# A one-core attention and Fourier-mixing kernel: a small addition moved from VectorE to GpSimd, and a few steps of a written-out order moved

## The chip, the cores and the metric

The kernel runs on one core of a Trainium2 chip. A core has TensorE (PE, matrix products into PSUM), VectorE (DVE), ScalarE (ACT), GpSimd (POOL) and SyncE (SP), each with its own queue that it works through in order, and 16 DMA engines. The metric is the time of one execution on the device, in microseconds. Before the change the median of three runs is 413.38 us (412.26 to 414.96).

## The reference

Inputs are q, k and v, each 8 batches x 8 heads x 576 rows x 64, a projection w_phi (64 x 128) and two weights of a feed-forward layer (512 x 2048 and 2048 x 512), all float32.

```python
def phi(x):
    proj = np.einsum('bhsd,df->bhsf', x, w_phi)
    proj = proj - np.max(np.abs(proj), axis=-1, keepdims=True)
    return np.concatenate([np.exp(proj), np.exp(-proj)], axis=-1)
q_p, k_p = (phi(q), phi(k))
kv = np.einsum('bhsf,bhsd->bhfd', k_p, v)
z = np.sum(k_p, axis=2)
num = np.einsum('bhsf,bhfd->bhsd', q_p, kv)
den = np.einsum('bhsf,bhf->bhs', q_p, z)[..., None] + 1e-06
x = (num / den)            # heads side by side: 8 x 576 x 512
mixed = np.real(fft(fft(x, axis=1), axis=2))
u = x + mixed
un = (u - mean(u)) / np.sqrt(var(u) + 1e-06)     # over the 512 columns
out = u + np.maximum(un @ w_ch1, 0.0) @ w_ch2
```

## The kernel before, in words

**Tiling.** A batch has 576 rows: chunks 0 to 3 of 128 rows and chunk 4 of 64 rows. k and q are loaded by GpSimd's DMAs (with a cast to bf16), transposed by DMAs that SyncE issues, and multiplied with w_phi on TensorE. ScalarE takes both exponentials of each product (KPp and KPn of keys, QPHP and QPHN of queries) out of PSUM, and VectorE takes the maxima of its absolute values (MK of keys, MQ of queries). In place of being subtracted, k's maximum is an exponential factor on v: ScalarE writes it into column 64 of VCn, VCp (and V4N, V4P of the 64 rows), and GpSimd multiplies v by it (lines 441 and 426).

TensorE then makes kv for each head and, for each head in the order 0, 1, 6, 7, 4, 5, 2, 3, the numerators and denominators (pn_, line 953). VectorE combines the two signs (tg, line 960, then cb, line 967) and takes a reciprocal per pair of heads (rd, line 971); GpSimd multiplies the pair into X (line 973). There are two cb buffers.

The Fourier transforms are products with sine and cosine tables, made small by symmetry: VectorE first folds X by rows into R (`folded`, lines 867 to 891), then by columns (CEO), TensorE multiplies twice (psD, pu), and VectorE adds the result to X. ScalarE writes X minus its mean into UN, SyncE's DMAs transpose that to UT, TensorE makes the hidden layer (psf, line 1211), ScalarE its relu HT (lines 1216 and 1218), TensorE the output (pso, lines 1228 and 1255), and VectorE adds it, times the row's scale, to X (lines 1234 and 1262). SyncE stores X to the output (lines 1187 to 1198).

**The row's scale.** `scales` makes 1/sqrt(var + 1e-6) for the five chunks of a batch from the variances in MV: VE is the sum (line 1170), rs its power of -0.5 (line 1171, GpSimd). For batch 0 this is done in two parts, so there are nine such pairs of instructions. rs is read by the updates at lines 1234 and 1262.

**PSUM.** The pool pj has two buffers, for psk (keys), psq and psh (queries), psD and pn_; the pool pb has three, for psf, pso, pu and others; the pool pk has one. A new tile waits until all readers of the one before it in its buffer are done. Where two engines read the same PSUM tile, the second one in program order waits for the first, as the waits in the rows below show.

**What sets the order.** The table PLAN is a string of letters, one for each step of a stream; `step` takes the letter's stream one `yield` further, and each engine's queue is filled in that order. Each stream goes through the batches on its own: F is the feed-forward part, M the heads and the mixing, D the row folds (its first step is the first two folds), N the normalisation, U the scales, P the maxima of q, T the projections with their exponentials, R the maxima of k (its first step is the 64 rows, then one for each pair of heads), S the scaled v, K, V and Q the loads, A the transposes of q, B those of k, O the stores (its steps are chunks 2, 1, 3 and 4). At any time several batches are in work: while F of batch 3 runs, M works on batch 4 and T on batch 5.

The fetch of v (`fetch_v`) has three steps: the two loads of the 64 rows (VS4), then two of 4 heads each. v has one buffer, k's and q's transposes have one each, X has three.

Of the kernel before, what the change touches and what calls it, by code (L numbers as in the profile page):

```python
# [10 lines left out]
ALU = mybir.AluOpType  # L11
# [15 lines left out]
    "MFPTMMFOTFSFMPTFFOPTTPMFFFFMFSNBFMFPTQMFFAFMNPFTFMNMFFMFFMMFTTFFURMFFVFRMFFSTFFMFFMFVFTTPFFOFFRFPDFF"  # L27
    "FTPFFFFFVDDRFFFQFDTMTFFKKQTSMFFFMFFFMRMFTTTMMFNNOFFMMFMFMFFSSMTFMTFFFNOFOSQTPPMFTFMBFPTFPAMFFFMFNTFK"
    "MMFFFNFMFMFFMFFUMQMFFVMFFFTTPFFFFMTFFRFTTFFOVFFFRFFRFDFFFFDFDFFDPTFMFTTFFFFMKFRFTMSFMRFFOMFTSPMFNTMP"
    "NSQFFFFQMMMMTTTFFOBMSFFFFOTPMTFSFFMFFMTPVMFFFFMTPNFFNNMMMFFMAFFFMUFMFKMFFFMFFTTDTTFRFFSFFFFRVFFOTMFF"  # L30
    "FFFRPTFFDFFFDRFFFTDFMFVKTPFFFFFMTMBQMFFRSFMFOTSTSTMMFFFNNSFMMFMMFTFMFOPTMKKFFFFOPTPMTFFMFFFNMFTPPMFF"
    "FTNFQMNMVFFMFQMFMFFMUFFMFFVMAFFFFTTTTFDRFRFFTFSFFFOFMRFFQFFFDFFTFFFDFFRFVDFTFMFFTTMFFMFFMFRSMFOQTTTM"
    "FTQFNFMSFFMFFTNPMMFOMSTPMTFFFFOSMTPPMFTFFMPPFBAFMFPFMFNNFMMVVFMFMFFFMTTFRMNUFFFFFMRFFFMFFFSTFFMFFPTF"
    "FOTFFFDDFFFRFTFFFDFDVRFFFMFTTFFMFMTMFRFFSMFFSFOMTTNTFFMFNMMFFFMMFTFOMPSTFNFFFOPTFMFFTMPFFFFMPSPMFFTM"
    "FFPFTMNFFFNMFMFFFUMFMFMFFFFMFFMFMFFFFOFDFFDFFFFFDFFFDFMFFFMFMFFMMFFMFNFMNFFOFFFFMFFFFOFMNFFFOMFFNFFF"
    "FFFFFFFFFFFFNUFFFFFFFFFFFFFFFFFFFFFFFFFFFFFFFFFFFFFFFFFFFFFFFFFFF"
# [4 lines left out]
def kernel(  # L41
# [10 lines left out]
    nc = tc.nc  # L52
# [1098 lines left out]
    def measure(b, c):  # L1151
        X, mv, _ = mixed[b]
        M = rows(c)
        st = small.tile([128, 6], F32, tag="st", name="st")
        nc.vector.bn_stats(out=st[0:M, :], in_=X[0:M, c, 0:C])  # L1155
        nc.vector.bn_aggr(out=mv[0:M, c, :], in_=st[0:M, :])  # L1156

    def scales(b):
        mv = mixed[b][1]
        for first, cs in ((True, slice(0, 3, 2)), (False, slice(0, 5))):  # L1160
            if b == 0:
                for c in (0, 2) if first else (1, 3, 4):
                    measure(b, c)
                    yield
            if b and first:
                continue
            n = 2 if first else 5
            rs = small.tile([128, n], F32, tag=f"rs{n}", name=f"rs{n}")
            VE = small.tile([128, n], F32, tag=f"VE{n}", name=f"VE{n}")
            nc.vector.tensor_single_scalar(out=VE[:], in_=mv[:, cs, 1], scalar=1e-06, op=ALU.add)  # L1170
            nc.gpsimd.tensor_tensor(out=rs[:], in0=VE[:], in1=mhalf[:, 0:n], op=ALU.pow)  # L1171
            for j, c in enumerate((0, 2) if first else range(5)):
                if b or first or c in (1, 3, 4):
                    scale_of[b, c] = rs[:, j:j + 1]
            yield
# [163 lines left out]
    def fold_later(b):  # L1339
        yield from folds[b]  # L1340

    STREAMS = {
        "F": (forward, 68), "M": (mixing, 26), "D": (fold_later, 4), "N": (normalise, 5),
        "U": (scales, 1), "P": (part(0), 7), "T": (part(1), 18), "R": (part(2), 5),
        "S": (part(3), 5), "K": (fetch_k, 2), "V": (fetch_v, 3), "Q": (fetch_q, 3),
        "A": (arrive, 1), "B": (arrive_k, 1), "O": (store_all, 4), "W": (load_ffn_weights, 2),
# [55 lines left out]
```

## Time and profile before

| | |
|---|---|
| median of three runs | 413.38 us (412.26 to 414.96) |
| the profiled execution | 413.93 us, of it 412.2 us span from its first to its last instruction |
| granted TensorE clock, mean | 0.989 |
| DMA traffic | 42.71 MB, 104 GB/s in the mean |

The profile is that of one execution. Engine rows give the start and the length of an instruction, or of several alike in a row (x2, x4), and in brackets how long the engine had been idle before and what ended that. Names stand as out<-in with buffer numbers left out. A matmul's length is that of a pipeline: several overlap.

### The profile page before, as it was taken

The page shows a single profiled execution, that of the slowest core. Times are in us where ns is not written, and L with a number is a line of the kernel's source. Part 1 is how long each engine was busy: PE and PEld are TensorE (multiplying, and loading weights), DVE is VectorE, ACT ScalarE, POOL GpSimd, SP SyncE. Part 2 cuts the span into 40 slices and gives each one's busy share as a digit, 9 for nine tenths or more (in the row PEclk, how much of TensorE's full clock was granted, in tenths as well). Part 3 has the DMA queues.
Part 4 walks back from the last instruction along what each step waited for, and adds up shares of the span by engine and source line. Part 5 has one row for each costly group of instructions (what it writes and reads, how often), then busy time and mean ns, then how long its engine had stood idle before and what let it go on. Part 6 is the DMA issues. An engine that isn't in the chain of part 4 may idle for free.

```text
span 412.2 us, 10494 instructions
## 1 busy us (share of the span) xinstructions
PE 392.6 (95%) x4165; PEld 260.1 (63%) x4194; DVE 319.9 (78%) x662; ACT 303.6 (74%) x617; POOL 214.5 (52%) x279
## 2 busy tenths in 40 slices
PE   6898999999999998999999999999989999999995
PEld 3574476545856576566856577566846587657564
DVE  5889887999699887798689869788789768966102
ACT  7788999668958895598968886889758886444350
POOL 8898785765466753707658474647452342201000
PEclk9899899999999999999999999999999999999999
DMA  8979979998574959763985959756993150106202
GB/s 225 234 125 165 173 97 195 86 122 140 101 119 59 109 106 133 97 99 78 106 126 76 154 95 154 76 65 113 117 102 52 29 100 21 26 4 113 60 25 65
DMA packets 108674, 42.71 MB, mean 104 GB/s; under 512 B 82769, under 2 KB 103633, under 8 KB 108625
## 3 DMA queue, kind: packets, MB, share of 16 engines
q0 software_dynamic: 46272, 16.60, 37.2%
q1 hardware_dynamic: 61905, 25.11, 33.4%
q8 instruction: 33, 0.54, 0.5%
q10 hardware_dynamic: 448, 0.33, 0.3%
q14 instruction: 16, 0.13, 0.1%
HBM read 36.77 MB, written 9.44 MB: 112 GB/s over the span
## 4 chain that ended last, share of the span: by engine, by line
PE 76%; DVE 16%; DMA 3%; POOL 2%; issue 1%; ACT 1%; DVEq 0%; POOLq 0%
PE psf L1211 29%; PE pso L1228 20%; PE kv L851 4%; PE pso L1255 3%; PE psD L1033 2%; DMA KT<-KS 2%; PE pu L1085 2%; PE psh L561 2%; PE psk L466 2%; PE psq L520 2%; DVE R L867 2%; DVE MK L486 1%; DVE cb L967 1%; PE idle L1333 1%; DVE tg L960 1%
## 5 line engine op out<-in xcount | busy, mean ns | idle before, releaser
L1211 PE MATMUL psf<-UT,W1b 128*128 128x320 bf16 (+1 forms) x1024 | 141.1, 286 | 0.4 <-DMA UT<-UN 0.3
L1228 PE MATMUL pso<-W2b,HT 128*128 128x512 bf16 x467 | 117.0, 379 | 1.8 <-issue 0.6
L1211 PEld LDWEIGHTS <-W1b 128*128 128x128 bf16 x1024 | 94.7, 98 | 28.1 <-issue 2.4
L1216 ACT ACTIVATE HT<-psf 128x320 bf16<-128x320 f32 x128 | 53.8, 443 | 25.6 <-PE psf L1211 19.5
L1228 PEld LDWEIGHTS <-HT 128*128 128x128 bf16 x496 | 45.2, 98 | 43.1 <-issue 0.4
L973 POOL TENSOR_TENSOR X<-cb,rd 128x640 f32<-128x640 f32 x28 | 35.1, 1254 | 46.4 <-DVE rd L971 19.5
L441 POOL TENSOR_TENSOR VCn<-VS,VCn 128x512 bf16<-128x512 bf16 x28 | 29.6, 1059 | 45.2 <-ACT VCn L436 40.0
L528 DVE TENSOR_REDUCE MQ<-psq 128x8 f32<-128x1024 f32 (+1 forms) x32 | 34.3, 1088 | 14.8 <-PE psq L520 14.4
L1234 DVE SCALAR_TENSOR_TENSOR X<-pso,rs,X 128x512 f32<-128x512 f32 x31 | 23.1, 744 | 28.2 <-PE pso L1228 28.0
L1218 ACT ACTIVATE HT<-psf 128x512 bf16<-128x512 f32 x64 | 37.4, 602 | 4.8 <-PE psf L1211 4.5
L486 DVE TENSOR_REDUCE MK<-psk 128x8 f32<-128x1024 f32 x28 | 33.8, 1210 | 1.4 <-ACT KPn L472 1.4
L472 ACT ACTIVATE KPp<-psk 128x1024 bf16<-128x1024 f32 x28 | 28.7, 1027 | 8.3 <-PE psk L466 8.2
L258 POOL DMA_DIRECT2D QS<-in_q_dram x49 | 33.5, 691 | 1.1 <-DMA QT<-QS 0.6
L1131 ACT ACTIVATE UN<-X,MV 128x512 bf16<-128x512 f32 (+1 forms) x35 | 25.2, 726 | 11.7 <-DVE MV L1156 8.1
L570 ACT ACTIVATE QPHP<-psh 128x1024 bf16<-128x1024 f32 x28 | 28.9, 1031 | 4.3 <-PE psh L561 4.0
L472 ACT ACTIVATE KPn<-psk 128x1024 bf16<-128x1024 f32 x28 | 28.7, 1024 | 2.1 <-DVE MK L486 2.1
L441 POOL TENSOR_TENSOR VCp<-VS,VCp 128x512 bf16<-128x512 bf16 x28 | 29.6, 1057 | 0.0
L570 ACT ACTIVATE QPHN<-psh 128x1024 bf16<-128x1024 f32 x28 | 29.0, 1034 | 0.0
L1155 DVE BATCH_NORM_STATS2 st<-X 128x6 f32<-128x512 f32 (+1 forms) x40 | 27.1, 678 | 0.2
L1075 DVE TENSOR_TENSOR X<-pu,X 128x512 f32<-128x512 f32 (+3 forms) x49 | 23.5, 526 | 4.9 <-PE pu L1085 4.8
L953 PEld LDWEIGHTS <-QPHP 128*128 128x128 bf16 x280 | 20.5, 98 | 9.3 <-DVE cb L967 5.5
L1171 POOL TENSOR_TENSOR rs<-VE,mhalf 128x5 f32<-128x5 f32 (+1 forms) x9 | 10.3, 1148 | 26.0 <-DVE VE L1170 25.7
(462 smaller groups left out, 798.7 us busy)
## 6 DMA issues: line engine op xcount, KB each, us to landing
out_dram<-X SPq DMA_DIRECT2D x16, 256.0 KB
KS<-in_k_dram POOLq DMA_DIRECT2D x7, 512.0 KB, 8.1
VS<-in_v_dram POOLq DMA_DIRECT2D x14, 256.0 KB, 4.8
out_dram<-X SPq DMA_DIRECT2D x28, 128.0 KB
W1b<-in_moe_w_ch_dram POOLq DMA_DIRECT2D x1, 2048.0 KB, 13.8
W2b<-in_moe_w_ch_dram POOLq DMA_DIRECT2D x1, 2048.0 KB, 15.6
QS<-in_q_dram POOLq DMA_DIRECT2D x28, 64.0 KB, 3.7
QS<-in_q_dram POOLq DMA_DIRECT2D x7, 256.0 KB, 7.6
```

The lines of the kernel that those rows point to most:

```text
L258: nc.gpsimd.dma_start(out=pieces[i][0], in_=pieces[i][1])
L441: nc.gpsimd.tensor_tensor(out=VC[:, hs, :, 0:D], in0=values[b][0][:, hs, :].rearrange("p h (j d) -> p h j d", d=D), in1=VC[:, hs, :, D:D + ...
L472: nc.scalar.activation(out=KP[:, hs, :, :].rearrange("p e (jp jj) f -> p jj (e jp) f", jj=2), in_=psk[:], func=AT.Exp, scale=sgn,)
L486: nc.vector.tensor_reduce(out=MK[:, 2 * pr:2 * pr + 2, :].rearrange("p e (jp jj) -> p jj (e jp)", jj=2), in_=tiles[pr][:], axis=AX.X, op=A ...
L528: nc.vector.tensor_reduce(out=o, in_=i[:], axis=AX.X, op=ALU.max, apply_absolute_value=True)
L570: nc.scalar.activation(out=o, in_=psh[:], func=AT.Exp, scale=sgn)
L973: nc.gpsimd.tensor_tensor(out=X[:, :, at:at + 2 * D].rearrange("p c (e d) -> p e c d", e=2), in0=cb[:, :, :, 0:D], in1=rd[:].to_broadcast( ...
L1155: nc.vector.bn_stats(out=st[0:M, :], in_=X[0:M, c, 0:C])
L1211: nc.tensor.matmul(ps, lhsT=W1b[:, cc, 128 * hh:128 * hh + 128], rhs=UT[:, cc, lo:hi], start=(cc == 0), stop=(cc == NCC - 1),)
L1216: nc.scalar.activation(out=HT[:, hh, lo:hi], in_=ps, func=AT.Relu, scale=-1.0)
L1218: nc.scalar.activation(out=HT[:, hh - 1:hh + 1, lo:hi], in_=psw[:].rearrange("p (a n) -> p a n", a=2), func=AT.Relu, scale=-1.0,)
L1228: nc.tensor.matmul(po[:], lhsT=HT[:, hh, at:at + 128], rhs=W2b[:, hh, :], start=(hh == 0), stop=(hh == NHH - 1),)
```

## The change

Nine small additions change their engine: line 1170, `scales`, goes from `nc.vector` to `nc.gpsimd`, so VE and rs now stand behind each other on GpSimd. The rest is in PLAN: six letters stand elsewhere.

- R's first two steps of batch 5 (maxima of the 64 rows and of the first pair of heads) stand ahead of D's first step of batch 4, and ahead of T's second exponential of the first pair.
- O's third step of batch 2 (store of chunk 3) stands behind B of batch 5 (transposes of k).
- O's third and fourth steps of batch 4 (stores of chunk 3 and of the 64 rows) stand behind B of batch 7.
- V's first step of batch 7 (the two loads of the 64 rows of v) stands in the middle of S of batch 6, two of whose steps follow it.

```diff
-    "NSQFFFFQMMMMTTTFFOBMSFFFFOTPMTFSFFMFFMTPVMFFFFMTPNFFNNMMMFFMAFFFMUFMFKMFFFMFFTTDTTFRFFSFFFFRVFFOTMFF"
+    "NSQFFFFQMMMMTTTFFBOMSFFFFOTPMTFSFFMFFMTPVMFFFFMTPNFFNNMMMFFMAFFFMUFMFKMFFFMFFTTRRDTTFFFSFFFFVFFOTMFF"
...
-    "FTQFNFMSFFMFFTNPMMFOMSTPMTFFFFOSMTPPMFTFFMPPFBAFMFPFMFNNFMMVVFMFMFFFMTTFRMNUFFFFFMRFFFMFFFSTFFMFFPTF"
+    "FTQFNFMSVFFMFFTNPMMFMSTPMTFFFFSMTPPMFTFFMPPFBOOAFMFPFMFNNFMMVFMFMFFFMTTFRMNUFFFFFMRFFFMFFFSTFFMFFPTF"
...
-            nc.vector.tensor_single_scalar(out=VE[:], in_=mv[:, cs, 1], scalar=1e-06, op=ALU.add)
+            nc.gpsimd.tensor_single_scalar(out=VE[:], in_=mv[:, cs, 1], scalar=1e-06, op=ALU.add)
             nc.gpsimd.tensor_tensor(out=rs[:], in0=VE[:], in1=mhalf[:, 0:n], op=ALU.pow)
```

GpSimd's queue at the scales of batch 3 (rs_3937 is read by F of batch 3, X is batch 4's, KS_3962 the 64 rows of batch 6's k), as a piece of the difference:

```order
 L973 TENSOR_TENSOR X<-cb,rd 128x2x5x64 [waits DVE_49]
-L1171 TENSOR_TENSOR rs_3937<-VE_3938,mhalf 128x5 [waits DVE_49]
-L258 DMA KS_3962<-in_k_dram 64x8x64 [waits DMAHW1_49]
+L1170 TENSOR_SCALAR VE_3938<-MV_112 128x5
+L1171 TENSOR_TENSOR rs_3937<-VE_3938,mhalf 128x5 [waits Pool_49]
```

The power waits for GpSimd's own addition now, and no longer for VectorE.

ScalarE's queue where T of batch 5 begins (psk is its first and then its second pair of heads, K4n the 64 rows):

```order
 L458 ACTIVATE K4n<-ps_4006 128x512
 L472 ACTIVATE KPp<-psk 128x2x4x128 [waits PE_49]
-L472 ACTIVATE KPn<-psk 128x2x4x128
-L472 ACTIVATE KPp<-psk 128x2x4x128 [waits PE_49]
-L422 ACTIVATE V4N<-MK_3901 64x4 [waits DVE_49]
-L422 ACTIVATE V4N<-MK_3901 64x4 [waits Activation_49]
+L472 ACTIVATE KPn<-psk 128x2x4x128 [waits DVE_49]
+L472 ACTIVATE KPp<-psk 128x2x4x128 [waits PE_49]
+L422 ACTIVATE V4N<-MK_3901 64x4 [waits Activation_49] x2
```

No instruction of ScalarE moves here, but KPn of the first pair has a wait for VectorE (the maximum that reads the same psk), and V4N has lost one. On VectorE the two maxima, lines 481 and 486, stand ahead of the two folds of line 867 and of both updates of line 1234, where they stood between these two.

SyncE's queue at batch 7's fetch (KT is k transposed, KT_5381 or KT_5380 its 64 rows, out_dram the stores of batch 4), as a piece of the difference:

```order
+L383 DMA_TRANSPOSE KT_5381<-KS_4445 128x4x64
+L385 DMA_TRANSPOSE KT<-KS 128x8x128 x2
 L1195 DMA out_dram<-X 4x32x512
 L1197 DMA out_dram<-X 63x512
 L1198 DMA out_dram<-X 1x512
-L383 DMA_TRANSPOSE KT_5380<-KS_4445 128x4x64
-L385 DMA_TRANSPOSE KT<-KS 128x8x128 x2
```

The three transposes of k stood behind the three stores and stand ahead of them now.

## Prediction

> **What bounds the kernel.** I read the page first, then TensorE's waits, then the timelines around each of its longer waits.
>
> ```profile
> PE 392.6 (95%) x4165; PEld 260.1 (63%) x4194; DVE 319.9 (78%) x662; ACT 303.6 (74%) x617; POOL 214.5 (52%) x279
> PE 76%; DVE 16%; DMA 3%; POOL 2%; issue 1%; ACT 1%; DVEq 0%; POOLq 0%
> ...
> PE pn__3170 L953 <- DVE cb L967: 1.8, 1, 1.8
> PE psk L466 <- DMA KT<-KS: 1.4, 1, 1.4
> PE pn__4074 L953 <- DVE MK L486: 0.6, 1, 0.6
> PE psf L1211 <- DMA UT<-UN: 0.3, 1, 0.3
> ```
>
> The first row gives busy time, the second the shares of the chain that ended last, the others who TensorE (PE) waited for: total, times, longest, in us. TensorE is busy 392.6 of 412.2 us, so the change, which takes no matmul away, can only win idle time of TensorE. The four rows are the idle pieces near the edits. They sum to 4.1 us, and that is the most that can be won. The sum is made on the profiled execution, 413.93 us, which lies 0.55 above the median of 413.38. What goes off the path there I take off the median.
>
> **The 1e-6 on GpSimd.** Nine small additions (line 1170) leave VectorE and stand on GpSimd ahead of the power (line 1171).
>
> ```profile
> L1170 DVE TENSOR_SCALAR VE<-MV 128x5 f32<-128x5 f32 x8 | 4.0, 497 | 0.1
> L1171 POOL TENSOR_TENSOR rs<-VE,mhalf 128x5 f32<-128x5 f32 x8 | 9.6, 1197 | 26.0 <-DVE VE L1170 25.7
> ...
> 162.07 1.96 DVE L1170 TENSOR_SCALAR VE<-MV 128x5 f32<-128x5 f32 x1
> 164.53 0.50 DVE L967 TENSOR_TENSOR cb<-pn__3126,tg 128x325 f32<-128x325 f32 x1
> 255.64 1.21 DVE L1170 TENSOR_SCALAR VE<-MV 128x5 f32<-128x5 f32 x1
> 161.51 2.47 POOL L973 TENSOR_TENSOR X<-cb,rd 128x640 f32<-128x640 f32 x2
> 165.95 2.40 POOL L258 DMA_DIRECT2D QS<-in_q_dram  x4 [0.64 <-DMA QT<-QS]
> 162.28 1.03 PE L1228 MATMUL pso<-W2b,HT 128*128 128x512 bf16 x4
> 165.08 0.20 PE L953 MATMUL pn__3170<-kvh,QPHP 128*128 128x65 bf16 x1 [1.77 <-DVE cb L967]
> 167.67 0.40 PE L520 MATMUL psq<-wphi,QT 64*128 64x128 bf16 x8
> ```
>
> Group rows end with busy us, mean ns and idle before; timeline rows begin with start and duration. Eight additions take 4.0 us, of which two take 1.96 and 1.21; the other six share 0.8, 0.14 each. The long one at 162.07 ends at 164.03, just when GpSimd's two products X end (161.51 + 2.47 = 163.98): a small VectorE instruction was held while GpSimd worked. Behind it stand tg and cb of pn__3126, and TensorE's pn__3170 needs the PSUM buffer that this cb frees.
>
> The Trainium skill ("SBUF — State Buffer", Who interferes with whom) says of such a hold that whoever of the two engines issues first has the shared ports for the whole instruction, and that the other waits until then. By that rule the addition, waiting since 162.07, would go when the first X ended (162.75) and be done at 162.9; 1.1 us less could then be won here, and the sum below would be -1.8. The row differs: it waited through the second X too, and the row decides.
>
> Without the addition tg begins at about 162.16. Its cb writes into the buffer that the first X has read (done at 161.51 + 1.24 = 162.75), so it runs from 162.8 to 163.3, and pn__3170 starts at 163.38, where TensorE has ended its four pso (162.28 + 1.03 = 163.31). That is 165.08 - 163.38 = **1.70 us**. Next in line is psq at 167.67, then 165.97: its transposed q has landed by 165.95, since the loads of q that overwrite its source start there. It fits, barely. The hold at 255.64 stands near no wait of TensorE, and neither do the six short ones: 0.
>
> What the addition costs on GpSimd no row shows. Bounds are the smallest copy and the power:
>
> ```profile
> 289.67 0.18 POOL L507 COPY MQ<-MQ 64x4 f32<-64x4 f32 x1
> ...
> DVE R L867 <- POOL X L973: 3.2, 3, 1.4
> ```
>
> 0.18 to 1.2 us, nearer to the copy in size and kind; I take 0.25. VectorE waited for GpSimd's X three times, the row folds R at line 867. The longest of these is at the next place, where the order of VectorE changes and covers it (below). At the upper price I allow one of the other two to reach TensorE: 0 to +1.2, taken as 0.
>
> **The two maxima ahead of the row folds.** Where batch 5's keys begin (span 213 to 221), MK of the 64 rows (line 481) and MK of the first pair of heads (line 486) pass R, batch 4's first fold.
>
> ```profile
> 214.03 1.29 DVE L867 TENSOR_TENSOR R<-X 128x512 f32<-128x512 f32 x2 [1.35 <-POOL X L973]
> 215.91 0.68 DVE L481 TENSOR_REDUCE MK<-ps 128x4 f32<-128x512 f32 x1
> 216.50 1.22 DVE L486 TENSOR_REDUCE MK<-psk 128x8 f32<-128x1024 f32 x1
> ...
> 213.15 0.59 ACT L458 ACTIVATE K4n<-ps 128x512 bf16<-128x512 f32 x1
> 213.62 1.03 ACT L472 ACTIVATE KPp<-psk 128x1024 bf16<-128x1024 f32 x1
> 214.53 1.04 ACT L472 ACTIVATE KPn<-psk 128x1024 bf16<-128x1024 f32 x1
> 216.62 0.46 ACT L422 ACTIVATE V4N<-MK 64x4 bf16<-64x4 f32 x2
> 217.59 1.02 ACT L472 ACTIVATE KPn<-psk 128x1024 bf16<-128x1024 f32 x1
> 218.84 2.61 ACT L1216 ACTIVATE HT<-psf 128x320 bf16<-128x320 f32 x5 [0.23 <-PE psf L1211]
> ...
> 213.32 3.83 PE L1228 MATMUL pso<-W2b,HT 128*128 128x512 bf16 x17 [0.16 <-issue]
> 217.78 0.20 PE L953 MATMUL pn__4074<-kvh,QPHP 128*128 128x65 bf16 x1 [0.62 <-DVE MK L486]
> ...
> 218.26 2.72 PE psf L1211 x20
> ```
>
> VectorE stood idle 1.35 us for X and then did R, an update and the maxima, so pn__4074 waited 0.62 for the buffer psk. Now the first maximum starts when K4n ends (213.74), the second when KPp ends (214.65), and it ends at 215.87; R follows at 215.9, with X at hand since 214.0, or 214.3 with the addition in front of it. So GpSimd's extra work is covered by up to 1.9 us.
>
> But the new order adds a wait: the second exponential KPn of the same psk now stands behind the maximum on ScalarE's queue. It starts at 215.87 instead of 214.53, 0.91 behind KPp's start. pn__4074 waits for it: done at 216.9, before TensorE is through with pso at 217.15. The 0.62 goes. Queued behind KPn, 0.91 each, are KPp of the next pair (216.8), four V4 (217.7, together 217.59 - 216.62 = 0.97), KPn (218.7) and then the first HT at 219.6; five HT take 2.61, so it is done at 220.1. TensorE, at 217.46 after pn__4074, does three psf in three PSUM buffers (0.54 each by the last row) until 219.09; the fourth needs the buffer that the first HT frees, and waits 1.0. The fifth ends at 220.1 + 2 x 0.54 = 221.2, where it ended at 218.26 + 2.72 = 220.98 before. So this place costs **+0.2**, with -0.6 (ScalarE catches up) and +0.6 (each of its pieces 0.1 longer) as ends.
>
> **Stores behind the K transposes, v sooner.** Both on batch 7's fetch, near 290.
>
> ```profile
> 283.31 2.94 SPq L1148 DMA_TRANSPOSE UT<-UN  x2
> 286.81 0.61 SPq L1195 DMA_DIRECT2D out_dram<-X  x1
> 289.55 1.45 SPq L383 DMA_TRANSPOSE KT<-KS  x1
> 291.14 3.55 SPq L385 DMA_TRANSPOSE KT<-KS  x2
> ...
> 285.06 4.16 DMA UT<-UN
> ...
> 291.14 9.44 DMA KT<-KS
> ...
> 285.45 1.06 POOL L441 TENSOR_TENSOR VCn<-VS,VCn 128x512 bf16<-128x512 bf16 x1 [2.09 <-ACT VCn L436]
> 290.17 2.10 POOL L258 DMA_DIRECT2D VS<-in_v_dram  x3 [0.16 <-issue]
> ...
> VS<-in_v_dram POOLq DMA_DIRECT2D x14, 256.0 KB, 4.8
> VS<-in_v_dram POOLq DMA_DIRECT2D x14, 32.0 KB, 5.8
> ```
>
> SyncE's three stores wait for the residual updates and hold the K transposes until 289.55. Without them the first goes at 283.31 + 2.94 = 286.25, and the first of the two large ones at 287.8 instead of 291.14. A transpose of half the size took 4.16 us to land here, and K's own 9.44 beside three loads of v; so it lands between 292.0 and 297.2, and TensorE asks for it at 300.58 - 1.38 = 299.2. **-1.38** at either end. The stores then go at about 291, with X's buffer not written again before batch 7's heads: 0. The same swap in batch 5's fetch, near 196, moves transposes that no wait of TensorE names: 0.
>
> Of v, the two loads of the 64 rows move into the 2.09 us in which GpSimd waited before 285.45 (two issues of 0.70), so the vector products are not held; the big load goes 1.4 sooner, at 290.17. What these loads may do is slow the UT transposes that land at 289.22 and for which TensorE waits 0.34: below, that wait goes (-0.34); above, it is the first rival's price. I take 0: the loads are small, but nothing is slack there.
>
> The sum: -1.70 + 0.2 - 1.38 = -2.88, so 411.05 for the profiled execution and **410.5** for the median.
>
> **Rivals.**
> - *v collides (slower).* UT's second transpose is issued at 285.06, and the loads of v now run beside it. If it takes the 9.44 us that K's took beside loads of v, it lands at 294.50, TensorE waits 5.6 in place of 0.34, and the sum is -2.88 + 5.28 = +2.4: 415.8. It turns slower from a landing of 4.16 + 2.88 = 7.0 us. For it: that row. Against: there 320 KB were loaded, here 64. 0.10. The Trainium skill ("DMA: Bandwidth & Descriptors", Issuing engines are not separate DMA queues) has DMAs of all issuing engines interleave on the same engines, which is this rival's mechanism; that K's transposes took 9.44 beside loads from another queue agrees.
> - *The hold at 162 stays in another form.* If cb gets its buffer only when both X are done (163.98), it ends at 164.5, pn__3170 starts near 164.6, and 0.5 is won, not 1.70: sum -1.7, 411.7. Much the same comes out if other executions hold the addition for one X only (1.1 less: -1.8). For it: the hold's length is a matter of a few tenths in two queues. Against: cb needs the first X alone, and the hold was seen in full. 0.20.
> - *All four waits go,* ScalarE losing nothing: -1.70 - 1.38 - 0.62 - 0.34 = -4.04, 409.3. Against it: three PSUM buffers and a queue of five exponentials. 0.15.
>
> **Chances and range.** The forecast has 0.50, from 409.9 (the low end of the maxima, -0.6) to 410.9; 0.05 is left for what I don't see. 1% is 4.1 us, about what can be told from no change, so faster by that is under 409.25: half of the last rival and a little, 0.09. Slower by 1% is beyond even the collision: 0.03. Within: 0.88. The range goes from 408.9 (409.3, less 0.4 for the spread of runs, 412.26 to 414.96) to 413.6 (411.7 with the addition's 1.2 and 0.7 of spread), and leaves out the collision.
>
> **What will show it.** Right: no VectorE addition, pn__3170 without a wait, a wait of about 1 us of psf on ScalarE's HT in the place of pn__4074's, KPn started by MK, no wait of psk for KT, and TensorE's busy time unchanged. Wrong: UT landing 7 us after issue, a new wait on cb near 163, or GpSimd's addition near 1.2 us with R late behind it.

## The result, and the profile after

The changed kernel takes 410.65 us in the median of 20 runs (409.41 to 412.16), the kernel before 412.98 beside it (20 runs, 410.85 to 414.96). The ratio is 0.9947, with a 95% interval of 0.9932 to 0.9963: 1.5 to 2.8 us faster. The forecast was 410.5. The profiled execution took 409.8 us (forecast 411.05), span 408.0.

The first row has the page's busy times; then come TensorE's waits (total, times, longest) and the added group on GpSimd.

```profile
PE 394.2 (97%) x4194; PEld 259.4 (64%) x4194; DVE 316.6 (78%) x653; ACT 302.8 (74%) x617; POOL 217.0 (53%) x288
...
PE psk L466 <- DMA KT<-KS: 1.6, 1, 1.6
PE psf L1211 <- ACT HT L1216: 0.9, 1, 0.9
PE pn__3170 L953 <- DVE cb L967: 0.2, 1, 0.2
...
L1170 POOL TENSOR_SCALAR VE<-MV 128x5 f32<-128x5 f32 x8 | 1.9, 239 | 25.0 <-DVE MV L1156 24.4
```

Of the four waits near the edits, pn__3170's has shrunk from 1.77 to 0.20, pn__4074's is gone, and psf's on HT is new. The psk row on KT is not batch 7's wait, which is gone: it ends at 40 us, in the first tenth of the program. GpSimd's addition takes 0.24.

The three places in the timelines of the changed kernel (start, length, idle before and what ended it); first the one at 162, then the maxima, then batch 7's fetch with the landing of UT from the chain.

```profile
159.82 0.72 POOL L258 DMA_DIRECT2D KS<-in_k_dram  x1 [9.09 <-DMA KT<-KS]
160.55 2.47 POOL L973 TENSOR_TENSOR X<-cb,rd 128x640 f32<-128x640 f32 x2
161.85 0.50 DVE L967 TENSOR_TENSOR cb<-pn__3126,tg 128x325 f32<-128x325 f32 x1 [0.44 <-POOL X L973]
162.41 0.20 PE L953 MATMUL pn__3170<-kvh,QPHP 128*128 128x65 bf16 x1 [0.20 <-DVE cb L967]
...
211.71 1.23 DVE L486 TENSOR_REDUCE MK<-psk 128x8 f32<-128x1024 f32 x1 [0.23 <-ACT KPp L472]
212.96 1.02 ACT L472 ACTIVATE KPn<-psk 128x1024 bf16<-128x1024 f32 x1 [1.29 <-DVE MK L486]
216.67 2.20 ACT L1216 ACTIVATE HT<-psf 128x320 bf16<-128x320 f32 x5
214.04 0.19 PE L953 MATMUL pn__4074<-kvh,QPHP 128*128 128x65 bf16 x1
217.15 1.25 PE L1211 MATMUL psf<-UT,W1b 128*128 128x320 bf16 x8 [0.94 <-ACT HT L1216]
...
285.74 2.64 SPq L385 DMA_TRANSPOSE KT<-KS  x2
296.37 0.40 PE L466 MATMUL psk<-wphi,KT 64*128 64x128 bf16 x8
...
282.45 3.95 DMA UT<-UN
```

The profiled spans differ by 4.2 us, more than the medians. About 1.3 of it is not the change's. ScalarE's order is the same in both kernels but for waits, so its instructions can be compared one by one; here is the same exponential early in the program (line 774) and the same one near 300 (line 472), before and then after.

```profile
14.39 1.02 ACT L774 ACTIVATE KPp<-psk 128x1024 bf16<-128x1024 f32 x1 [1.28 <-PE psk L768]
306.79 1.02 ACT L472 ACTIVATE KPn<-psk 128x1024 bf16<-128x1024 f32 x1 [0.90 <-DVE MK L486]
```

```profile
13.07 1.03 ACT L774 ACTIVATE KPp<-psk 128x1024 bf16<-128x1024 f32 x1
302.62 1.02 ACT L472 ACTIVATE KPn<-psk 128x1024 bf16<-128x1024 f32 x1 [0.45 <-DVE MK L486]
```

The changed kernel is 1.32 us ahead at 14 us, where nothing is changed (before, psk of line 768 waited 2.0 for KT; after, 0.9), and 4.17 at 306.79. Between them lie 2.85 us, beside a forecast sum of 2.88. That this agrees so well is partly luck: from 47 to 160 us the lead is 1.1, so the places from there on gained 3.1. Compared instruction by instruction, these are 1.59 at pn__3170, 0.31 right behind it, -0.41 at the maxima, 0.21 near 290 (psf waits 0.13 for UT, and 0.34 before) and 1.35 at batch 7's keys.

The 0.31 is not in the forecast sum. Before, VectorE was idle for 0.46 us ahead of the cb of pn__3170, and psq started 0.53 behind the last psk ahead of it (167.14) and 0.15 behind the end of that cb. After, the gap is 0.10, and psq starts 0.23 behind psk. The cb before, then cb and psq after:

```profile
167.02 0.50 DVE L967 TENSOR_TENSOR cb<-pn__3170,tg 128x325 f32<-128x325 f32 x1 [0.46 <-DVE tg L960]
```

```profile
164.00 0.50 DVE L967 TENSOR_TENSOR cb<-pn__3170,tg 128x325 f32<-128x325 f32 x1
164.69 0.39 PE L520 MATMUL psq<-wphi,QT 64*128 64x128 bf16 x8
```

The gap of 0.46 is there in all seven profiled kernels with the additions on VectorE, wherever they stand, and in none of the four with them on GpSimd (without the probes). In six of the seven psq is 0.3 late behind it; in the seventh (below, at 165) TensorE itself is behind. What VectorE waits for there no profile shows: tg, which the row names, had ended.

### The profile page after: what moved, and what is told of

Its sections match the earlier page's. It is cut to its first block, busy times and chain, and to the rows that moved or that the text cites. A ratio compares the mean times of both kernels' runs of the same rounds, so it can differ in the third digit from the quotient of the medians.

```text
span 408.0 us, 10522 instructions
## 1 busy us (share of the span) xinstructions
PE 394.2 (97%) x4194; PEld 259.4 (64%) x4194; DVE 316.6 (78%) x653; ACT 302.8 (74%) x617; POOL 217.0 (53%) x288
## 3 DMA queue, kind: packets, MB, share of 16 engines
HBM read 36.77 MB, written 9.44 MB: 113 GB/s over the span
## 4 chain that ended last, share of the span: by engine, by line
PE 76%; DVE 10%; DMA 6%; ACT 5%; POOL 1%; issue 1%; POOLq 0%; SPq 0%; DVEq 0%; ACTq 0%
PE psf L1211 28%; PE pso L1228 22%; DMA KT<-KS 3%; PE kv L851 3%; PE pso L1255 3%; PE psD L1033 2%; PE idle L1333 2%; PE pu L1085 2%; PE psh L561 2%; PE psk L466 2%; PE psq L520 2%; DMA KS<-in_k_dram 2%; DVE MK L486 1%; DMA UT<-UN 1%; PE pso L1275 1%; DVE cb L967 1%
## 5 line engine op out<-in xcount | busy, mean ns | idle before, releaser
L1228 PE MATMUL pso<-W2b,HT 128*128 128x512 bf16 x496 | 120.5, 379 | 0.0
L867 DVE TENSOR_TENSOR R<-X 128x512 f32<-128x512 f32 x32 | 20.3, 685 | 2.7 <-POOL X L973 2.6
```

The source lines that it names most:

```text
L1228: nc.tensor.matmul(po[:], lhsT=HT[:, hh, at:at + 128], rhs=W2b[:, hh, :], start=(hh == 0), stop=(hh == NHH - 1),)
```

## The experiments

Each kernel ran on one chip beside the kernel before, and its ratio is against the runs of that kernel there. Differences of TensorE's waits are read from one profile each.

**The additions alone on GpSimd.** The order stays as before.

```diff
-            nc.vector.tensor_single_scalar(out=VE[:], in_=mv[:, cs, 1], scalar=1e-06, op=ALU.add)
+            nc.gpsimd.tensor_single_scalar(out=VE[:], in_=mv[:, cs, 1], scalar=1e-06, op=ALU.add)
```

> Only the nine additions go to GpSimd; the order stays as before. Theory (VectorE's addition was held by GpSimd's products): the 1.77 us that pn__3170 waited for cb near 163 falls to about 0.2, nothing of it comes back later, and the time is 1.6 us under the kernel before (about 0.4%). The other three waits stay: psk on KT near 300 about 1.4, pn__4074 on MK about 0.6, psf on UT about 0.3. Rival (the wait only moves): psq near 166 or pn__4074 grows by more than half a us, and the gain is 0 to 0.5 us.

411.51 us (12 runs) beside 413.04, ratio 0.9958 (0.9931 to 0.9985). The size in time came out, but of the four waits only psf's for UT (0.28) is as expected:

```profile
159.97 0.72 POOL L258 DMA_DIRECT2D KS<-in_k_dram  x1 [9.54 <-DMA KT<-KS]
160.71 2.47 POOL L973 TENSOR_TENSOR X<-cb,rd 128x640 f32<-128x640 f32 x2
162.56 0.20 PE L953 MATMUL pn__3170<-kvh,QPHP 128*128 128x65 bf16 x1 [0.65 <-DVE cb L967]
211.84 1.29 DVE L867 TENSOR_TENSOR R<-X 128x512 f32<-128x512 f32 x2 [1.90 <-POOL X L973]
215.58 0.20 PE L953 MATMUL pn__4074<-kvh,QPHP 128*128 128x65 bf16 x1 [1.10 <-DVE MK L486]
296.90 0.40 PE L466 MATMUL psk<-wphi,KT 64*128 64x128 bf16 x8
```

pn__3170 still waits 0.65, because the first X, whose end cb needs, comes late. GpSimd's load of KS stands ahead of X and waits for K's transposes to land. pn__4074 waits 1.10 and not 0.62: GpSimd's addition delays the X of that place, and R and the maxima behind it. From the X ahead of the addition to the X behind it, 3.64 us pass on GpSimd (206.90 to 210.54) and 3.15 before: 0.49 more, of which the addition's own row is 0.24. And psk did not wait for KT here, though nothing near it was moved.

**The maxima alone.** R's first two steps of batch 5 ahead of D's.

```diff
-FMFFTTDTTFRFFSFFFFRVFFOTM
+FMFFTTRRDTTFFFSFFFFVFFOTM
```

> Only the two maxima go ahead of the row folds. Theory: pn__4074's wait of 0.62 us is gone, and a wait of psf for HT of 0.9 to 1.0 us stands 3 us behind it, because the second exponential KPn waits for the maximum: the time is 0.2 to 0.3 us above the kernel before, which can hardly be told from no change; the two waits in the trace decide. Rival (ScalarE makes it up): no wait of psf, 0.6 us faster.

412.76 us (12 runs) beside 413.04, ratio 0.9988 (0.996 to 1.0016): no change that can be told. pn__4074 does not wait, psf waits 0.9 for HT. Matched with before, this execution is 0.21 ahead just ahead of the place; then KPn is 1.21 behind and the HT 0.60, 0.38 and 0.15 behind: a loss of 0.36. The two waits say the same (0.94 for 0.62). The theory held.

**The stores behind K's transposes alone, in batch 7's fetch.**

```diff
-TNPMMFOMSTPMTFFFFOSMTPPM
+TNPMMFMSTPMTFFFFSMTPPM
...
-FMPPFBAFMFPF
+FMPPFBOOAFMFPF
```

> Only the stores of chunk 3 and of the 64 rows go behind the K transposes of batch 7; the loads of v, the additions and the maxima stay as before. Theory: K's transposes land near 292, TensorE's wait of psk for KT near 300 (1.38 us) is gone, and the time is 1.4 us under the kernel before. Rival (the stores, or the transposes that now start beside UT's, make another wait): psf's wait for UT grows beyond 0.34 by a us or more, and the gain is under 0.5 us.

411.58 us (12 runs) beside 413.04, ratio 0.9964 (0.9937 to 0.9991), 1.46 less. K's two large transposes landed 3.19 and 3.71 us after their issue, psk waited for nothing, and psf waited 0.2 for UT. The theory held. Its profile shows something else at 162, where the addition is still on VectorE:

```profile
160.81 0.71 POOL L258 DMA_DIRECT2D KS<-in_k_dram  x1 [10.24 <-DMA KT<-KS]
160.82 0.12 DVE L1170 TENSOR_SCALAR VE<-MV 128x5 f32<-128x5 f32 x1
161.54 2.47 POOL L973 TENSOR_TENSOR X<-cb,rd 128x640 f32<-128x640 f32 x2
162.84 0.50 DVE L967 TENSOR_TENSOR cb<-pn__3126,tg 128x325 f32<-128x325 f32 x1 [1.50 <-POOL X L973]
163.39 0.20 PE L953 MATMUL pn__3170<-kvh,QPHP 128*128 128x65 bf16 x1 [1.33 <-DVE cb L967]
```

The addition was not held at all in this execution (0.12), and pn__3170 waited 1.33 all the same. So my theory of this wait fell short: the hold is one way in which a late X reaches TensorE, cb's wait for its buffer is the other. Both may come from the load ahead of X; the next experiment tries that.

**That load behind the two X, with the addition still on VectorE.** K's first step of batch 5 goes behind M's that issues the second X.

```diff
-FMFNTFKMMFFFN
+FMFNTFMMFFFN
...
-MFMFFMFFUMQM
+MFMFFMKFFUMQM
```

> The kernel before, with one thing moved: GpSimd's load of the 64 rows of batch 5's k (KS), which stood ahead of the two products X near 161 and waited 9 us for K's transposes, stands behind them; the addition stays on VectorE. Theory (the load is what put X on top of the addition, and what still makes cb wait when the addition has left): the first X starts as soon as rd is there, 1.4 us sooner, the addition at 162 falls between the two X or waits for the second only, cb finds its buffer free, and pn__3170's wait of 1.3 to 1.8 us falls to 0 to 0.3 with the addition still on VectorE: 1.3 to 1.7 us under the kernel before. Rival (the hold of the addition alone counts, and it meets an X wherever the load stands): the addition takes over 1 us again, and pn__3170 still waits 0.7 us or more.

410.56 us (6 runs) beside 413.28, ratio 0.9926 (0.9903 to 0.995): 2.7 less, more than the 1.3 to 1.7 expected.

```profile
159.95 1.25 POOL L973 TENSOR_TENSOR X<-cb,rd 128x640 f32<-128x640 f32 x1 [8.35 <-DVE rd L971]
161.86 0.12 DVE L1170 TENSOR_SCALAR VE<-MV 128x5 f32<-128x5 f32 x1
162.02 1.25 POOL L973 TENSOR_TENSOR X<-cb,rd 128x640 f32<-128x640 f32 x1 [0.82 <-DVE VE L1170]
162.48 0.50 DVE L967 TENSOR_TENSOR cb<-pn__3126,tg 128x325 f32<-128x325 f32 x1
163.03 0.20 PE L953 MATMUL pn__3170<-kvh,QPHP 128*128 128x65 bf16 x1
```

Without the load ahead of it, X waits only for rd, the addition falls between the two, cb and pn__3170 wait for nothing. Matched with before, the place gains 1.84; the other 0.9 of this execution are shorter waits for UT and KT near 290 and 300, where nothing was moved. The nine moved additions gained 1.3, 1.3 and 1.9 between 160 and 200 us (alone, with the maxima split, in the changed kernel), psq's 0.31 counted in: one letter does about as much.

**The additions on VectorE, but right behind the last variance of each batch.**

```diff
+                if c == 4:
+                    wide[b] = widen(mv[:, :, 1], 5)
...
-            nc.vector.tensor_single_scalar(out=VE[:], in_=mv[:, cs, 1], scalar=1e-06, op=ALU.add)
+            VE = wide[b] if b else widen(mv[:, cs, 1], n)
```

(`widen` makes the same addition on VectorE.)

> The kernel before, with the additions of batches 1 to 7 still on VectorE but issued right behind the last variance of their batch, some 3 us earlier near 158, where GpSimd computes nothing. Theory (a hold by GpSimd, not the addition's own work, cost the time): the addition takes 0.12 to 0.16 us, pn__3170 waits 0.2 to 0.8 us (as where the additions went to GpSimd, since cb still waits for the first X), and pn__4074 waits 0.6 as before and not 1.1, since GpSimd has nothing more to do: 1.0 to 1.6 us under the kernel before. Rival (any VectorE addition there delays cb): pn__3170 waits 1.3 us or more and the time is that of before.

410.85 us (6 runs) beside 413.28, ratio 0.9939 (0.9914 to 0.9963). The addition at 158.58 took 0.17; cb waited 0.28 for X, pn__3170 not at all, which is less than expected, and pn__4074 0.62. So it was the meeting with GpSimd that cost, not the addition's own work. The first X is as late as before here (161.41, behind the same load), and with the hold gone that alone did not reach TensorE. The profile has the longest wait for K's transposes of all:

```profile
298.71 0.40 PE L466 MATMUL psk<-wphi,KT 64*128 64x128 bf16 x8 [1.63 <-DMA KT<-KS]
```

In the five executions with stores and loads of v in the old order this wait was 1.38 (before), 0 (additions alone), 0.81 (maxima alone), 0.83 (load behind X) and 1.63: 0.93 in the mean. With the transposes ahead of the stores it was 0 in all five.

**The parts costed at nothing.** The first step of batch 7's v sooner, and B ahead of the store in batch 5's fetch.

```diff
-MTTTFFOBMSFFFF
+MTTTFFBOMSFFFF
...
-QFNFMSFFMFFT
+QFNFMSVFFMFFT
...
-FNNFMMVVFMFMF
+FNNFMMVFMFMF
```

> The kernel before with the two parts that were costed at nothing: the loads of the 64 rows of batch 7's v sooner, and the store of chunk 3 behind the K transposes of batch 5. Theory: no wait of TensorE changes at either place (none at 196, psf on UT 0.1 to 0.4 near 289), the time is that of the kernel before within 0.3%. Rival (the loads of v beside UT's second transpose): UT lands over 5.5 us after its issue, psf waits 1.5 us or more, slower by that.

411.80 us (12 runs) beside 413.79, ratio 0.9958 (0.9931 to 0.9985): 2.0 faster (0.6 to 2.9), not 0. UT landed 4.27 us after its issue and psf waited 0.45, so nothing collided. psk did not wait for KT: the second of K's three transposes landed 7.87 us after its issue, beside 9.44 before, with one load of v near it and not three. That can be worth the 0.9 of the mean above; but with the additions alone that transpose landed after 7.76, beside three loads, so one profile does not show that the loads are the reason. Where the rest of the 2.0 came from, if there is more, this profile, which is the longest of its runs (414.17 us), does not show. It shows a loss of its own at 165:

```profile
165.25 0.20 PE L953 MATMUL pn__3170<-kvh,QPHP 128*128 128x65 bf16 x1 [2.00 <-DVE cb L967]
165.64 2.75 PE L1228 MATMUL pso<-W2b,HT 128*128 128x512 bf16 x6
...
165.00:167.00 2.00, 1.75 (x14) 0.91 (x15) 1.67 (x5) 0.00 (x0) 1.47 (x3) 0.62 0.98 195
167.00:169.00 2.00, 2.00 (x16) 0.71 (x16) 0.50 (x1) 0.00 (x1) 1.98 (x4) 0.53 1.06 114
```

The last two rows are stretches of 2 us, with the busy time of the five engines and then the granted clock. After a wait of 2.00 the clock falls to 0.53, and six pso take 2.75, where they took 1.46 before behind a wait of 1.77.

**The maxima split.** The changed kernel, with the maximum of the 64 rows ahead of the folds and that of the first pair behind them and behind KPn.

```diff
-MFFTTRRDTTFFFSF
+MFFTTRDTRTFFFSF
```

> The changed kernel, with the maximum of the 64 rows ahead of the row folds as there, and that of the first pair behind the folds and behind both exponentials of the pair. Theory: KPn starts right behind KPp (0.9 later, not 2.3), so HT is in time and psf does not wait; the maximum follows the folds and ends within 0.2 us of the end of pso, so pn__4074 waits 0 to 0.2. Both waits are gone: 0.7 to 0.9 us under the changed kernel, 3.0 to 3.3 under the kernel before. Rival (the order of the maxima does not matter, ScalarE is late for another reason): psf still waits 0.9 us for HT and the time is that of the changed kernel.

410.28 us (8 runs) beside 413.04, ratio 0.9918 (0.9888 to 0.9948).

```profile
212.10 1.04 ACT L472 ACTIVATE KPn<-psk 128x1024 bf16<-128x1024 f32 x1
213.31 1.22 DVE L486 TENSOR_REDUCE MK<-psk 128x8 f32<-128x1024 f32 x1
215.80 2.45 ACT L1216 ACTIVATE HT<-psf 128x320 bf16<-128x320 f32 x5
214.58 0.19 PE L953 MATMUL pn__4074<-kvh,QPHP 128*128 128x65 bf16 x1
```

KPn starts 0.90 behind KPp (211.20), HT is in time, and neither pn__4074 nor psf waits. Matched with before, the place gains 0.54, where the changed kernel loses 0.41. The trace bears the theory out; the time, 0.4 below the changed kernel by the medians, can't be told from it.

**The best kernels.** The split maxima, with the load behind the X as above; and the same with the additions back on VectorE.

> The changed kernel with the maximum of the first pair behind the folds and both exponentials, and GpSimd's load of KS behind the two products X near 161. Theory: pn__3170 does not wait at all (it waited 0.2 to 0.8 in the runs with the additions on GpSimd, for an X that stood behind this load), nor does psf near 216 or psk near 300: 0.5 us under the kernel with the split maxima alone, 2.8 to 3.6 under the kernel before. Rival (the load goes later and its data are late, or the wait moves to psq): 0 or slower than the split maxima alone.

> The kernel with split maxima and KS's load behind the two X, but the 1e-6 stays on VectorE. Theory (once the load is out of the way of the X, where the addition stands is worth nothing): the addition near 162 takes 0.12 us, pn__3170 does not wait, and the time is within 0.3 us of the same kernel with the additions on GpSimd. Rival (the additions still meet an X, near 255 or 162, and TensorE feels it): 0.5 us or more slower than that.

409.79 us (6 runs), ratio 0.9911 (0.9887 to 0.9935), and with VectorE's additions 409.15 us (6 runs), ratio 0.9897 (0.9853 to 0.9941), on another chip. In both, none of pn__3170, pn__4074 and the psk near 300 waits. The two intervals overlap; matched with before, the one moves from 0.14 us ahead at 47 to 4.52 at 307, the other from 1.02 to 5.11, the same gain but for 0.3. So once the load is out of the way, the engine of the additions makes no difference that the times can tell; the 0.3 is that of psq, behind the gap of 0.46. Both intervals also overlap the changed kernel's: that they beat it rests on the waits, not on the times.

**Why two products held the addition.** Three probes behind the kernel's end, each of GpSimd products of 128x640 and one small VectorE instruction that is ready while the first of them runs.

```diff
+            for i in range(n):
+                nc.gpsimd.tensor_tensor(out=xs[:, at:at + 640], in0=xs[:, 0:640], in1=xs[:, 0:640], op=ALU.mult)
+            nc.vector.tensor_single_scalar(out=pv[:], in_=pa[:], scalar=1e-06, op=ALU.add)
```

> The changed kernel with ten rounds of a probe behind its end: in each, GpSimd makes a small product (128x5), then 1, 2 or 4 products of 128x640 float32 back to back, and VectorE one small instruction of 128x5 that needs only the small product: an addition of a constant (one input), a sum of two inputs, or a maximum. Theory (a waiting VectorE instruction that needs what GpSimd holds gets no turn between GpSimd's instructions): the addition takes about 1.2, 2.4 and 4.9 us beside 1, 2 and 4 products, the maximum about 0.1 in any case; for the sum of two inputs I expect the same as for the addition. Rival (it gets its turn when the first product ends): 1.2 us whatever the number. The time of the whole run says nothing.

The addition beside one, two and four products (GpSimd's four shown), then the maximum:

```profile
404.71 1.20 DVE L1385 TENSOR_SCALAR pv<-pa 128x5 f32<-128x5 f32 x1 [0.31 <-POOL pa L1377]
406.22 1.20 DVE L1385 TENSOR_SCALAR pv<-pa 128x5 f32<-128x5 f32 x1 [0.31 <-POOL pa L1377]
408.80 1.20 DVE L1385 TENSOR_SCALAR pv<-pa 128x5 f32<-128x5 f32 x1 [1.38 <-POOL pa L1377]
422.87 0.16 DVE L1389 TENSOR_REDUCE pv<-pa 128x5 f32<-128x5 f32 x1 [3.80 <-POOL pa L1377]
...
408.72 4.88 POOL L1380 TENSOR_TENSOR px<-px 128x640 f32<-128x640 f32 x4
```

1.20 whatever the number: the addition went when the first product ended, and my theory fell. The sum of two inputs took 1.20 as well, the maximum 0.16 at once. (In the very first round the product was over before VectorE came.)

> The changed kernel with nine rounds of a second probe behind its end. The first probe showed 1.20 us for any number of products; the kernel before held its addition for 1.96 us through two. Three differences are tried: GpSimd's product in the kernel's own form (second input broadcast) or plain; the addition ready at the first product's start, or some 0.6 us later (a VectorE maximum of 500 elements ahead of it); and a second product that itself waits for a VectorE reciprocal issued just ahead of the addition. Theory A (what arrives in the middle of a product misses its end when the next product is queued): 1.8 us with two products and 4.2 with four when late, 1.2 otherwise. Theory B (the form of the product decides): 2.4 with two of the broadcast form, late or not. Rival (always the end of the running product): 1.2 at the start, 0.6 late, in every round. The time of the whole run says nothing.

In every late round the addition ended with the running product (0.49 to 0.61), in the others with the first (1.20; but for the first round, which GpSimd came to late); form, lateness and a second product with a wait of its own made no difference.

> The changed kernel with seven rounds of a third probe behind its end. In the second, the addition always ended with the product that was running (0.49 to 0.61 us when late), while the kernel before held it through two. What is left of the difference is tried: the addition's input read with a stride of two elements, as the kernel reads its variances, and a load issued by GpSimd just ahead of the products, as there. All rounds are late, with a second product that waits for a reciprocal. Theory A (the stride): about 1.8 us in the strided rounds with two products, 4.2 with four, 0.5 in the others. Theory B (the load's issue): 1.8 in the rounds with a load. Rival (neither): 0.5 to 0.6 in every round, and the hold through two products stays unexplained. The time of the whole run says nothing.

A round without and one with a load issued by GpSimd ahead of the products:

```profile
410.61 0.49 DVE L1408 TENSOR_SCALAR pv<-pa 128x5 f32<-128x5 f32 x1
424.93 1.70 DVE L1408 TENSOR_SCALAR pv<-pa 128x5 f32<-128x5 f32 x1
...
423.22 0.73 POOL L1384 DMA_DIRECT2D KS<-in_k_dram  x1
424.13 1.26 POOL L1401 TENSOR_TENSOR px<-pc,rone 128x640 f32<-128x640 f32 x1
425.35 1.25 POOL L1401 TENSOR_TENSOR px<-pc,rd 128x640 f32<-128x640 f32 x1
```

With the load ahead, the addition lasts to 426.63, past the end of the second product (426.60), in all three rounds of this kind (1.70 each), with a strided input or not; without it, 0.49 to 0.61. This fits the hold of 1.96 in the kernel before, where the KS load stands right ahead of the X; why a load does this no run shows.

## Why the prediction was right, step by step

- **The median and the interval** came out: 410.65 for 410.5. The profiled execution took 409.8 and not 411.05: its start was 1.3 ahead, and the places gained 3.1 for the forecast 2.88, with parts that differ from the sum's: psq's 0.31 and UT's 0.21 are not in it, and the loss at the maxima is twice as large. Two terms were read from one execution, too, and in others they are smaller. So the closeness is in part luck.
- **The addition off VectorE, -1.70.** The steps were right: cb ran as soon as the first X had ended (161.85), and pn__3170 followed, with 0.20 of wait left, 1.57 won. What failed is that I took the first X's start for given. It follows K's transposes, through the load ahead of it on GpSimd's queue, whose wait of 9 us I had not quoted. In the three executions with that load in place and the additions on GpSimd, 0.20, 0.65 and 0.76 remain; with the additions early on VectorE, nothing. What remains goes with the start: at 150 us these four led the kernel before by 1.09, 1.40, 1.10 and 0.08, but their load went only 0.97, 0.82, 0.41 and 0.11 sooner, so in the first three X was late for a VectorE that was ahead. In the four with the old order of both the wait was 1.77, 1.63, 1.33 and 2.00; the 1.33 is the one with such a lead (1.24). The means, 0.54 and 1.68, make this term about -1.1; it is about -0.8 with the lead and -1.8 without. psq, which I named as next in line and barely in time, gained another 0.31. It had followed cb and not the landing of q, and no term has it; it also shows that the four waits quoted were not the most that could be won.
- **The hold and the rule beside it.** I let the row of 1.96 decide against the Trainium skill ("SBUF — State Buffer", Who interferes with whom), by which the engine that issues first has the shared ports for one whole instruction. For this place the row was right; as a rule it was not. The probes agree with the skill (1.20 beside one, two and four products, 0.16 for the maximum) as long as no load is issued right ahead of the products, and show 1.70 where one is. The forecast did not hang on it, since without the addition there is nothing to hold.
- **GpSimd's addition, 0.25 and at no cost.** Its row is 0.24, but the X behind it comes 0.49 later. That the new order of VectorE covers this was right: that X is done at 211.51, and R follows the maximum at 212.85 with no wait for it. Where the order stays, the additions alone cost 0.48 at pn__4074 (1.10 for 0.62).
- **The maxima, +0.2.** Measured by the waits +0.32 (0.94 for 0.62), matched with before +0.41 in the changed kernel and +0.36 alone, by the mechanism forecast: KPn behind MK, HT late, the fourth psf waiting. Beside additions on GpSimd the same step is a small gain, 0.94 for 1.10.
- **K's transposes, -1.38.** Right in direction and, by luck, in size (1.35; the two large transposes landed 3.21 and 5.12 us after their issue); but the price is 0.93 in the mean of five executions, from 0 to 1.63, because the landing varies.
- **UT and v, 0.** UT landed 3.95 us after its issue, psf waited 0.13 until 286.45; the first rival, the collision, did not come. But "0" was too cautious for v: alone with batch 5's swap it made the time 0.4% shorter, perhaps in part through the transposes of K that it leaves alone. As psk waits for KT in neither profile, its and the stores' gains don't add up, nor do those of all the single runs (1.5, 0.3, 1.5 and 2.0 us against 2.3 for the whole).
- **The other rivals.** The hold did not stay in another form in the profile of the change, but a wait of cb for the late X did in two other executions, 0.45 and 0.56 longer than in this profile, where that rival had put 1.2. Not all four waits went: psf's came in as forecast.

An estimate from the figures above, -1.1 - 0.3 + 0.4 - 0.9 = -1.9, lies inside the measured 1.5 to 2.8. What may lie between it and the median's 2.3 is the clock: a wait of 2 us at 163 can cost some 1.5 us more in the matmuls behind it, and the change shortens that wait. One profile shows that; how often it happens in the kernel before was not measured.

## What to carry to other kernels

When an instruction waits for another engine, follow that engine's queue one step further: what delayed GpSimd's product was a load's wait for a DMA, and moving that load by a few places removed the whole stall in three executions of three. Moving the held instruction to another engine left 0.2 to 0.8 us of it in three; moving it forward on its own engine left nothing in the one seen. A wait that ends with a DMA's landing has a spread (here 0 to 1.6 us), so price it from several executions. A kernel's PSUM tile read by two engines passes a delay from one to the other in program order: put the reader that the other engine's queue waits for first, and the maximum behind both exponentials.

## What the runs showed of the hardware

- A small VectorE addition (128x5, float32) that is ready during a GpSimd product ends with that product, but with the product after it when GpSimd has issued a load right ahead: 1.70 and not 0.49 us in the same place. A maximum of the same size is not held (0.16).
- A wait of TensorE of 2.00 us at 163 was followed by 4 us at a granted clock of 0.53 to 0.62; waits of 1.77, 1.63 and 1.33 at the same place were not. Near 40 us it is the other way round: behind 1.63 (the changed kernel) and 1.86 (the maxima split) the clock fell to 0.50 and 0.56 in a stretch of 2 us, and behind 2.26 (split maxima, load behind X, additions on VectorE) it stayed at 1.00. So the length of a wait alone does not decide. The Trainium skill ("TensorE: Matmul & The Clock Gate", What's actually happening) has a free-running window of about 3.4 us decide this, with the lower clock after an idle one; all these waits are shorter than that window.
- In nine of the ten other profiled kernels (without the probes), the start lay 1.3 to 1.5 us ahead of the kernel before's at 14 us, with nothing changed there, and four of them had lost 1.1 to 1.2 of it again at 24: profiles are compared from a point behind such a difference.
